# First sweep: two sums and two turns head a batch's mixing step, first-layer units from slot 5 on

## The chip, the cores and the metric

One Trainium2 chip, one core. The metric is the device time of one execution in microseconds (us). The kernel before takes 1207.25 us (median of three runs, 1206.75 to 1207.27). A measurement of this kernel tells apart about 0.2%.

## What is computed

Causal attention with a decay (8 batches, 8 heads, 576 positions, head width 64), then a mixer over its output: a sum along the sequence through `U` and `V` (rank 32), and a two-layer perceptron 512 to 2048 to 512 with a residual. Everything is float32.

```python
scores = scale * q @ k.T + (cum[:, None] - cum[None, :])   # causal mask
x  = softmax(scores) @ v                                   # heads side by side: (8, 576, 512)
u  = x + (x.T @ U @ V).T
out = u + relu(u @ w_ch1) @ w_ch2
```

## The kernel before, in words

**Two sweeps.** The first sweep (lines 778 to 946) does all of attention, pair of heads by pair of heads, and mixes in the first 6 of the 16 blocks of hidden channels of the perceptron (`NA = 6`). The second sweep, from line 950, does the other ten blocks from `ud`, a copy of `u` in DRAM. float32 operands of the large products are split in a high part (a cast, on ACT) and a low part (a subtraction, on DVE), and each product is three matmuls.

**Steps and slots.** The first sweep is a list of steps `t` (0 to 33), one for each of the 32 pairs of heads and two to run out; pair `p` is scored in step `p`. `step(t)` (L822) writes 10 slots `s`. Slots 0 to 3 and 6 to 9 hold a score tile each (`S14_02` is pair 14, head 0, row block 2), slots 4 and 5 the tail scores `St`; beside them stand the transposes of the exponentials of the pair before (`T`, slots 0 to 2 and 5 to 8), the product with the values (`V`, slots 0 and 7), and small ones (`Tx` slot 3, `Ty` slot 4, `Tt` slot 8). The order on PE and SP is as written; DVE, ACT and POOL are ordered by the scheduler when the program is built.

**Units.** A batch `b` has its last attention output at the end of step 4b+5. Step 4b+6 is its *mixing step* (`MIX`, L820): each slot pops one unit of `mix_units(b)` (L650), five sums `H` (`x + TS VV`, a 512-column matmul, added to `x` by DVE, L664), then four turns `Tu` and `Tv` (transposes of `u`; ACT copies the high half `uh`, L667, DVE subtracts for the low half `ul`, L668). The perceptron's units (`ffn_units`, L705) are the *filler*: first layer `A` (12 matmuls, L723; relu on ACT to `hh`, L732, low half `hl` on DVE, L728) and second layer `B` (6 matmuls, L742; three units to a sum, then added to `x` by DVE, L757). There are 24 units for an even batch and 27 for an odd one, in two groups of columns. The first group needs only the turns `Tu` 0 and 1. Six units are left over (`held`, L775) and run in slots 0 to 4 of the next mixing step; the others run in slots 1 to 6, 8 and 9 (`ROOM`, L936) of the three steps behind a mixing step, dealt out evenly by `credit` (L914 to L920).

**Banks.** `H`, `Tu`, `Tv`, `A` and `B` share the two banks of the pool `psF` (L107); a unit that opens a bank waits until the tile that held it was read for the last time: `H` by DVE (L664), `Tu` by ACT and then DVE (L668), `A` by ACT and then DVE (L728), `B` by DVE (L757). A `B` tile keeps its bank over three units, so that the units beside it have the other bank alone. The score tiles share the two banks of `psS` in turn: `S14_02` waits until ACT has read `S14_00` (the exponential `P14_00`, L394).

**When the evacuations are written.** `defer(phase, fn, slots)` (L266) puts them in the list of a later slot, by phase within it; ACT and DVE then get them in the scheduler's order.

Of the kernel before, what the change touches and what calls it, by code (L numbers as in the profile page):

```python
# [8 lines left out]
F32 = mybir.dt.float32  # L9
# [4 lines left out]
ALU = mybir.AluOpType  # L14
# [3 lines left out]
B, H, S, D = 8, 8, 576, 64  # L18
# [22 lines left out]
def tile_decay_attention_moe(ctx, tc, qk, v, f, U, V, w1, w2, out):  # L41
    nc = tc.nc
# [218 lines left out]
    filler = []  # L261
# [3 lines left out]

    def defer(phase, fn, slots=1):  # L266
        later.setdefault(now[0] + slots, []).append((phase, fn))

    def run_later():
        now[0] += 1  # L270
        for _, fn in sorted(later.pop(now[0], []), key=lambda x: x[0]):
            fn()

    def run_filler():
        w, fn = filler.pop(0)
        fn()
        return w
# [366 lines left out]
    fine = [0]  # L644
    share = [0.0]

    def charge(us):
        share[0] -= us

    def mix_units(b):  # L650
        X = xn[b % NX]
        units = []

        def bank(name):

            if b == B - 1:
                return psS.tile([P, 512], F32, tag="S", name=name)
            return psF.tile([P, 512], F32, tag="F", name=name)

        def hmix(i):  # L660
            kk = P if i < NM else TAIL
            ps = bank(f"H{b}_{i}")
            nc.tensor.matmul(ps[0:kk], VV[:, P * i : P * i + kk], TSb[b], start=True, stop=True)
            defer(4, lambda: (charge(0.6), nc.vector.tensor_tensor(X[0:kk, i], ps[0:kk], X[0:kk, i], op=ALU.add)))  # L664

        def evac_u(dh, dl, src):
            defer(3, lambda: nc.scalar.copy(dh, src))  # L667
            defer(1, lambda: (charge(0.6), nc.vector.tensor_tensor(dl, src, dh.bitcast(F32), op=ALU.subtract)), 2)  # L668

        def tu(i):  # L670
            if i == 0 and b % 2 == 0:
                cur[0] = sf.tile([P, NDC, 640], F32R, tag="uh", name=f"uh{b}")
                cur[1] = sf.tile([P, NDC, 640], F32R, tag="ul", name=f"ul{b}")
            uh, ul = cur
            tp = bank(f"Tu{b}_{i}")
            for c in range(NDC):
                nc.tensor.transpose(tp[:, P * c : P * c + P], X[:, i, P * c : P * c + P], ident)
            sl = slice(P * i, P * i + P)
            evac_u(uh[:, :, sl], ul[:, :, sl], tp.rearrange("p (c t) -> p c t", c=NDC))

        def tv():
            uh, ul = cur
            to = MAIN if b % 2 else MAIN + TAIL
            tp = bank(f"Tv{b}")
            for c in range(NDC):
                nc.tensor.transpose(tp[:, 64 * c : 64 * c + 64], X[0:64, NM, P * c : P * c + P], ident[0:64, 0:64])
            tv_ = tp[:, 0:256].rearrange("p (c t) -> p c t", c=NDC)

            evac_u(uh[:, :, to : to + TAIL], ul[:, :, to : to + TAIL], tv_)

            def use():
                for x, t in enumerate((uh, ul)):
                    if b < B - 1:
                        nc.sync.dma_start(ud[b, :, x], t.bitcast(F32)[:, :, 0:MAIN])
                    if b % 2:
                        jt = b // 2
                        nc.sync.dma_start(ud[B, :, x, :, P * jt : P * jt + P], t.bitcast(F32)[:, :, MAIN : MAIN + P])

            defer(4, use, 2)

        h = [(0.43, lambda i=i: hmix(i)) for i in range(NM + 1)]
        t = [(0.43, lambda i=i: tu(i)) for i in range(NM)] + [(0.25, tv)]
        return h + t

    def ffn_units(b):  # L705
# [3 lines left out]
        for t0, nt in groups:  # L709
            g = {}  # L710

            def l1(fc, t0=t0, nt=nt, g=g):
                uh, ul = cur
                if fc == 0:
                    g["hh"] = sf.tile([P, NA, 384], F32R, tag="hh", name=f"hh{b}_{t0}")
                    g["hl"] = sf.tile([P, NA, 384], F32R, tag="hl", name=f"hl{b}_{t0}")
                hh, hl = g["hh"], g["hl"]
                sl = slice(t0, t0 + nt)
                ps = psF.tile([P, 512], F32, tag="F", name=f"A{b}_{t0}_{fc}")
                m = 0  # L720
                for c in range(NDC):
                    for wt, ut in ((w1h, uh), (w1l, uh), (w1h, ul)):
                        nc.tensor.matmul(ps[:, :nt], wt[:, fc, c], ut[:, c, sl], start=m == 0, stop=m == 3 * NDC - 1)  # L723
                        m += 1

                def low():
                    charge(nt / 768)
                    nc.vector.scalar_tensor_tensor(  # L728
                        hl[:, fc, :nt], ps[:, :nt], 0.0, hh.bitcast(F32)[:, fc, :nt], op0=ALU.max, op1=ALU.subtract
                    )  # L730

                defer(3, lambda: nc.scalar.activation(hh[:, fc, :nt], ps[:, :nt], AF.Relu), 1 + fine[0])  # L732
                defer(1, low, 2 + fine[0])

            def l2(x, part, t0=t0, g=g):
                hh, hl = g["hh"], g["hl"]
# [38 lines left out]
    def held(t):  # L775
        return 4 if t > MIX[-2] else 6
# [36 lines left out]
    mixing = []  # L813
# [5 lines left out]
    LAST = len(SEQ) - 1  # L819
    MIX = [SEQ.index(NHP * b + NHP - 1) + 3 for b in range(B)]  # L820

    def step(t):  # L822
# [11 lines left out]
        for s in range(6 + 2 if last else SLOTS):  # L834
# [26 lines left out]
            if (t, s) in DECODES:  # L861
                u = DECODES.index((t, s))
# [42 lines left out]
            if px and s == (6 if last else 8):  # L905
                ranks(c)

            if mixing:
                for _ in range(2 if t == MIX[0] and s < 3 else 1):
                    mixing.pop(0)[1]()  # L910
                for _ in range(1 if ending else (1, 1, 2, 1, 1)[s] if s < 5 else 0):
                    if filler:
                        run_filler()
            elif len(filler) > held(t) and s in ROOM:  # L914

                ahead = sum(x >= s for x in ROOM) + len(ROOM) * (min(m for m in MIX if m > t) - 1 - t)
                credit[0] += (len(filler) - held(t)) / max(ahead, 1)
                if credit[0] > 0.999 or t > LAST - 3:
                    credit[0] = max(credit[0] - 1, 0)
                    run_filler()  # L920
            if ps_ and s == 6:
                score(p, 1, 0)
# [2 lines left out]
            if px and s == (6 + 1 if last else 9) and st[c]["hp"] == NHP - 1:  # L925
                b = st[c]["b"]
                assert len(filler) <= held(t) and not mixing
                mixing.extend(mix_units(b))
                nxt = ffn_units(b)
                pending.append(nxt)  # L930
            if not mixing and pending:
                assert not filler
                filler.extend(pending.pop())

    pending = []
    ROOM = (1, 2, 3, 4, 5, 6, 8, 9)  # L936
    credit = [0.0]
# [79 lines left out]
    for k, (_, _, _, joined, power, rest, whole, high, _) in enumerate(stages):  # L1017
        ahead = stages[k + 1][0:3] if k + 1 < len(wb) else ()
# [19 lines left out]
    with tc.manual_schedule(engines={ET.PE, ET.DVE, ET.Activation, ET.SP}):  # L1038
# [12 lines left out]
        h, t = ([fn for _, fn in x] for x in (mixing[0 : NM + 1], mixing[NM + 1 :]))  # L1051
        mixing = []
# [105 lines left out]
    ends = sf.tile([P, 2 * HT], F32, tag="TS", name="sum2")  # L1158
# [200 lines left out]
    held = {}  # L1359
# [289 lines left out]
```

## Time and profile before

| what | value |
|---|---|
| runs, device time | 1206.75, 1207.25, 1207.27 us |
| profiled execution, first to last instruction (span) | 1205.1 us; its device time isn't given, the median run is 2.15 us above the span |
| PE (matmul) busy | 1183.8 us, 98% of the span |
| DVE, ACT, POOL busy | 931.2 us (77%), 767.3 us (64%), 514.8 us (43%) |
| granted clock of TensorE | 1.00 in every slice |
| chain that ended last, by engine | PE 83%, DVE 8%, ACT 6% |

How to read it: a matmul's end is modelled, so a row's duration on PE overlaps the next one's; the time that PE spends on something is read from start to start. A gap that the view shows as idle is shorter than the time lost, by what the modelled end hides.

### The profile page before, as it was taken

The page shows a single profiled execution, that of the slowest core. Times are in us where ns is not written, and L with a number is a line of the kernel's source. Part 1 is how long each engine was busy: PE and PEld are TensorE (multiplying, and loading weights), DVE is VectorE, ACT ScalarE, POOL GpSimd, SP SyncE. Part 2 cuts the span into 40 slices and gives each one's busy share as a digit, 9 for nine tenths or more (in the row PEclk, how much of TensorE's full clock was granted, in tenths as well). Part 3 has the DMA queues.
Part 4 walks back from the last instruction along what each step waited for, and adds up shares of the span by engine and source line. Part 5 has one row for each costly group of instructions (what it writes and reads, how often), then busy time and mean ns, then how long its engine had stood idle before and what let it go on. Part 6 is the DMA issues. An engine that isn't in the chain of part 4 may idle for free.

```text
span 1205.1 us, 23859 instructions
## 1 busy us (share of the span) xinstructions
PE 1183.8 (98%) x8460; PEld 1084.9 (90%) x8460; DVE 931.2 (77%) x2233; ACT 767.3 (64%) x2076; POOL 514.8 (43%) x506
## 2 busy tenths in 40 slices
PE   8999999999999999999999999999999999999998
PEld 5888898998998988989989997788999999999998
DVE  8987878778778678877686699976777867778675
ACT  8877786776868758767766577434454544545543
POOL 2215463553635435544442000024575555555553
PEclk9999999999999999999999999999999999999999
DMA  5754244335335325425322244533424344243420
GB/s 161 192 139 146 81 104 155 103 82 160 84 89 169 102 69 152 121 69 172 90 79 90 97 144 160 159 105 94 134 86 110 101 133 134 96 115 99 132 52 36
DMA packets 81159, 138.47 MB, mean 115 GB/s; under 512 B 8752, under 2 KB 45616, under 8 KB 78992
## 3 DMA queue, kind: packets, MB, share of 16 engines
q1 hardware_dynamic: 79824, 128.56, 35.4%
q0 software_dynamic: 1152, 8.39, 3.8%
q8 instruction: 67, 1.10, 0.4%
q14 instruction: 52, 0.43, 0.1%
q10 hardware_dynamic: 64, 0.00, 0.0%
HBM read 101.08 MB, written 35.78 MB: 114 GB/s over the span
## 4 chain that ended last, share of the span: by engine, by line
PE 83%; DVE 8%; ACT 6%; issue 1%; POOL 0%; ACTq 0%; DVEq 0%; POOLq 0%
PE N L1283 12%; PE A L723 12%; PE B L742 11%; PE A L1263 9%; PE B L1263 7%; PE V L564 5%; PE T L461 4%; PE S L365 3%; PE V L536 3%; PE S L366 2%; PE B L1283 2%; PE Tt L630 2%; PE S L362 2%; PE O L1348 1%; ACT G L328 1%
## 5 line engine op out<-in xcount | busy, mean ns | idle before, releaser
L394 ACT ACTIVATE P<-S,nm 128x128 f32<-128x128 f32 (+3 forms) x256 | 139.0, 545 | 54.5 <-DVE nm L386 48.8
L197 POOL TENSOR_TENSOR hb<-xn,hb 128x256 fp32r<-128x256 f32 x136 | 113.6, 856 | 125.5 <-ACT hb L194 108.0
L386 DVE CUSTOM_DVE_ANT_0 S<-S,mask 128x128 f32<-128x128 f32 (+3 forms) x256 | 125.8, 496 | 52.3 <-PE S L366 46.3
L328 POOL CAST G<-qk 64x576 fp32r<-64x576 f32 x52 | 35.4, 680 | 206.9 <-PE St L366 150.4
L723 PE MATMUL A<-uh,w1h 128*128 128x256 f32 (+1 forms) x384 | 119.7, 312 | 0.0
L723 PE MATMUL A<-ul,w1h 128*128 128x256 f32 (+1 forms) x384 | 113.6, 296 | 0.0
L723 PE MATMUL A<-uh,w1l 128*128 128x256 f32 (+1 forms) x384 | 113.5, 296 | 0.0
L194 ACT CAST hb<-xn 128x256 fp32r<-128x256 f32 x136 | 51.8, 404 | 77.3 <-DVE xn L1269 42.8
L443 DVE TENSOR_TENSOR PTl<-T,PTh 128x512 fp32r<-128x512 f32 (+1 forms) x156 | 79.0, 527 | 12.1 <-ACT PTh L440 11.1
L742 PE MATMUL B<-w2h,hh 128*128 128x512 f32 x216 | 88.2, 408 | 0.0
L461 PE MATMUL T<-ident,P 128*128 128x128 f32 x544 | 85.5, 273 | 0.0
L344 POOL TENSOR_TENSOR G<-qk,G 64x576 fp32r<-64x576 f32 x52 | 74.6, 1434 | 24.6 <-ACT G L328 24.3
L742 PE MATMUL B<-w2l,hh 128*128 128x512 f32 x216 | 85.0, 394 | 0.0
L742 PE MATMUL B<-w2h,hl 128*128 128x512 f32 x216 | 84.6, 392 | 0.0
L1283 PE MATMUL N<-sw,hb 128*128 128x256 f32 x546 | 80.4, 283 | 0.0
L1283 PE MATMUL N<-b2h,hb 128*128 128x256 f32 x420 | 79.9, 282 | 0.0
L343 POOL TENSOR_TENSOR G<-qk,G 64x576 fp32r<-64x576 f32 x52 | 75.0, 1442 | 10.9 <-issue 4.2
L365 PE MATMUL S<-G 128*128 128x128 f32 x208 | 70.8, 345 | 7.0 <-ACT P L394 5.8
L723 PEld LDWEIGHTS A<-uh,w1h 128*128 128x128 f32 x384 | 72.9, 190 | 0.9 <-DVE hl L728 0.2
L723 PEld LDWEIGHTS A<-uh,w1l 128*128 128x128 f32 x384 | 73.1, 190 | 0.5
L723 PEld LDWEIGHTS A<-ul,w1h 128*128 128x128 f32 x384 | 72.8, 190 | 0.0
L1283 PEld LDWEIGHTS N<-sw,hb 128*128 128x128 f32 x546 | 71.7, 190 | 0.4 <-POOL hb L197 0.2
(328 smaller groups left out, 4006.3 us busy)
## 6 DMA issues: line engine op xcount, KB each, us to landing
qk<-in_qk_dram SPq DMA_DIRECT2D x104, 288.0 KB
direct<-ud SPq DMA_DIRECT2D x48, 256.0 KB
sr<-in_w_dram SPq DMA_DIRECT2D x20, 512.0 KB
vr<-in_v_dram SPq DMA_DIRECT2D x32, 256.0 KB
accd<-ost SPq DMA_DIRECT2D x32, 256.0 KB
xn<-accd SPq DMA_DIRECT2D x8, 1024.0 KB
out_dram<-xn SPq DMA_DIRECT2D x32, 256.0 KB
ud<-uh SPq DMA_DIRECT2D x7, 1024.0 KB
```

The lines of the kernel that those rows point to most:

```text
L197: leng.tensor_tensor(dl, src, dh.bitcast(F32), op=ALU.subtract)
L343: pin(el.tensor_tensor(g[oth, 2, cols], k[oth], gf[oth, 2, cols], op=ALU.subtract))
L344: pin(em.tensor_tensor(g[own, 1, cols], q[own], gf[own, 0, cols], op=ALU.subtract))
L365: nc.tensor.matmul(ps, G[j][:, 0, c0 : c0 + P], G[j][:, 2, cols], start=first, stop=False)
L386: newest["top"] = nc.vector.tensor_tensor_reduce(ps[:, :w], ps[:, :w], mask[:, 512 - w : 512], scale=-SCALE, scalar=3.0e38, op0=ALU.add, o ...
L394: nc.scalar.activation(pt, ps[:, :w], AF.Exp, bias=z["nm"][:, col : col + 1], scale=-1.0, accum_out=z["sm"][:, col : col + 1])
L443: defer(2, lambda: nc.vector.tensor_tensor(dstl, src, dsth.bitcast(F32), op=ALU.subtract))
L461: nc.tensor.transpose(tp[:, P * x : P * x + P], z["P"][j][i][:, P * c : P * c + P], ident)
L723: nc.tensor.matmul(ps[:, :nt], wt[:, fc, c], ut[:, c, sl], start=m == 0, stop=m == 3 * NDC - 1)
L742: nc.tensor.matmul(ps, ht[:, fc, P * x : P * x + P], wt[:, fc], start=fc == 0 and m == 0, stop=fc == NA - 1 and m == 2,)
L1263: nc.tensor.matmul(ps, a[x][:, c], b[y][:, c], start=start and m == 0, stop=m == 5, skip_group_check=not start)
L1283: nc.tensor.matmul(ps[:, y], a[p_][:, P * y : P * y + P], w[q_], start=start and y == 0 and m == 0, stop=stop and y == 1 and m == 2,)
```

## The change

The first 1008 matmuls of PE's order and all from number 4437 (of 8236) on stand as before; between them the same instructions stand in another order. `mix_units` orders the units of batches 1 to 6 as `H` 0, 1, `Tu` 0, 1, `H` 2, 3, 4, `Tu` 2, 3, `Tv`. The batch's perceptron units come into the filler behind slot 4 of its mixing step, and the slots 5, 6, 8, 9 of that step may take one each (`packed`). In those slots the low halves (`evac_u`, `l1`) are deferred a slot less, in phase 3. `credit` deals the units over the room of the mixing step's second half and the three steps behind it.

```diff
+    packed = [False]
+
+    def soon(slots, fn):
+        defer(*(3, fn, slots - 1) if packed[0] else (1, fn, slots))
+
...
         def evac_u(dh, dl, src):
             defer(3, lambda: nc.scalar.copy(dh, src))
-            defer(1, lambda: (charge(0.6), nc.vector.tensor_tensor(dl, src, dh.bitcast(F32), op=ALU.subtract)), 2)
+            soon(2, lambda: (charge(0.6), nc.vector.tensor_tensor(dl, src, dh.bitcast(F32), op=ALU.subtract)))
...
         t = [(0.43, lambda i=i: tu(i)) for i in range(NM)] + [(0.25, tv)]
+        if 0 < b < B - 1:
+            return h[0:2] + t[0:2] + h[2:] + t[2:]
         return h + t
...
-                defer(1, low, 2 + fine[0])
+                soon(2 + fine[0], low)
...
+            packed[0] = t in MIX[1:] and s > 4
             if mixing:
...
-            elif len(filler) > held(t) and s in ROOM:
-
-                ahead = sum(x >= s for x in ROOM) + len(ROOM) * (min(m for m in MIX if m > t) - 1 - t)
-                credit[0] += (len(filler) - held(t)) / max(ahead, 1)
-                if credit[0] > 0.999 or t > LAST - 3:
-                    credit[0] = max(credit[0] - 1, 0)
+            if (packed[0] or not mixing) and len(filler) > held(t) and s in ROOM:
+
+                ends = [6 if u == LAST else 9 for u in range(t, min(m for m in MIX if m > t))]
+                ahead = sum(x <= end and (n > 0 or x >= s) for n, end in enumerate(ends) for x in ROOM)
+                credit[0] += (len(filler) - held(t)) / ahead
+                if credit[0] > 0.999:
+                    credit[0] -= 1
                     run_filler()
...
-            if not mixing and pending:
+            if pending and (not mixing or (t, s) in [(m, 4) for m in MIX[1:]]):
                 assert not filler
                 filler.extend(pending.pop())
```

Units by slot, before and after, for batches 2 and 3 (an even and an odd one; `A`, `B` with a group's letter a or b, then the block or the row tile; `-` is a slot without a unit). Batches 4 and 6 go as 2 in the mixing step, 5 as 3; batch 1 as 3, but with its third `A` behind `Tv` in slot 9.

```text
step 14 before  H0+Bb0 | H1+Bb0 | H2+Bb0+Bb1  | H3+Bb1  | H4+Bb1 | Tu0   | Tu1   | Tu2 | Tu3    | Tv
step 14 after   H0+Bb0 | H1+Bb0 | Tu0+Bb0+Bb1 | Tu1+Bb1 | H2+Bb1 | H3+A0 | H4    | Tu2 | Tu3+A1 | Tv+A2
step 15 before  - | A0 | A1 | A2 | - | A3 | A4 | - | A5 | -
step 15 after   - | -  | A3 | -  | A4 | A5 | - | - | Ba0 | Ba0
step 16 before  - | Ba0 | Ba0 | Ba0 | - | Ba1 | Ba1 | - | - | Ba1
step 16 after   - | -   | Ba0 | Ba1 | - | Ba1 | Ba1 | - | - | Ab0
step 17 before  - | Ab0 | Ab1 | -   | Ab2 | Ab3 | Ab4 | - | - | Ab5
step 17 after   - | -   | Ab1 | Ab2 | -   | Ab3 | Ab4 | - | - | Ab5
step 18 after   H0+Bb0 | H1+Bb0 | Tu0+Bb0+Bb1 | Tu1+Bb1 | H2+Bb1 | H3+A0 | H4+A1 | Tu2 | Tu3+A2 | Tv
step 19 after   - | A3 | A4 | A5 | - | Ba0 | Ba0 | - | - | Ba0
```

Slot 1 of steps 15, 16, 17, 23, 24 and 25 held a unit and holds none; slot 1 of step 8, in front of the place from which the order differs, holds none in either.

**ACT, slots 2 to 4 of mixing step 14** (`P` exponentials, `PTh` high halves of turned exponentials, `uh` high half of a turn). Before:

```order
L440 CAST PTh13_3553<-T13_v_3606 128x128
L394 ACTIVATE P14_02_3631,sm14_3524<-S14_02_3603,nm14_3523 128x384
L394 ACTIVATE P14_03_3656,sm14_3524<-S14_03_3639,nm14_3523 128x512
L500 CAST PT413_3555<-Ty13_12_3669 64x128
L614 CAST xh12_3688<-xn0_104 128x640
```

After:

```order
L445 CAST PTh13_3553<-T13_v_3606 128x128
L399 ACTIVATE P14_02_3636,sm14_3524<-S14_02_3603,nm14_3523 128x384
L672 CAST uh2_3610<-Tu2_0_3612 128x4x128
L399 ACTIVATE P14_03_3665,sm14_3524<-S14_03_3644,nm14_3523 128x512
L672 CAST uh2_3610<-Tu2_1_3652 128x4x128
L505 CAST PT413_3555<-Ty13_12_3678 64x128
```

The high half of each of the first two turns now stands behind an exponential. `B1_256_1`, whose first unit ends slot 2, takes the bank that `Tu2_0` leaves; `H2_2` in slot 4 the one that `Tu2_1` leaves.

**DVE, slots 8 and 9 of mixing step 14** (`ISA ... nm14` the row minima of a score tile, `xT` the sum of the two halves of `V`, `ul` and `hl` low halves). Before:

```order
L386 ISA S14_12_3782,nm14_3523<-S14_12_3782,mask_93 128x384
L386 ISA nm14_3523 128x1
L584 TENSOR_TENSOR xT13_3755<-V13_0_3754,cr13_0_3756 64x576
L668 TENSOR_TENSOR ul2_3703<-Tu2_2_3768,uh2_3702 128x4x128
L443 TENSOR_TENSOR PTl13_3554<-T13_12_3785,PTh13_3553 128x256
L443 TENSOR_TENSOR PTl13_3554<-T13_12_3785,PTh13_3553 128x128
L386 ISA S14_13_3822,nm14_3523<-S14_13_3822,mask_93 128x512
```

After, from the same place:

```order
L391 ISA S14_12_3800,nm14_3523<-S14_12_3800,mask_93 128x384
L391 ISA nm14_3523 128x1
L589 TENSOR_TENSOR xT13_3773<-V13_0_3772,cr13_0_3774 64x576
L673 TENSOR_TENSOR ul2_3611<-Tu2_2_3786,uh2_3610 128x4x128
L448 TENSOR_TENSOR PTl13_3554<-T13_12_3803,PTh13_3553 128x256
L448 TENSOR_TENSOR PTl13_3554<-T13_12_3803,PTh13_3553 128x128
L642 TENSOR_TENSOR TS3_3807<-Tt12_3808,TS3_3807 32x128
L673 TENSOR_TENSOR ul2_3611<-Tu2_3_3818,uh2_3610 128x4x128
L391 ISA S14_13_3855,nm14_3523<-S14_13_3855,mask_93 128x512
L391 ISA nm14_3523 128x1
L735 SCALAR_TENSOR_TENSOR hl2_0_3715<-A2_0_1_3823,hh2_0_3714 128x256
L673 TENSOR_TENSOR ul2_3611<-Tv2_3858,uh2_3610 128x4x64
```

`A1` (`A2_0_1`) in slot 8 takes the bank of `Tu2_2`, and `A2` in slot 9 that of `A1`, whose low half stands behind the row minima of `S14_13`. In the odd batches `A1` follows `H4` in slot 6 and takes `H4`'s bank.

**PE, slots 1 and 2 of step 16.** Before:

```order
L461 MATMUL T15_01_4184<-ident_99,P15_03_3963 128x128
L742 MATMUL B2_0_0_4188<-w2h_109,hh2_0_3887 128x512
L742 MATMUL B2_0_0_4188<-w2h_109,hl2_0_3888 128x512
L742 MATMUL B2_0_0_4188<-w2l_110,hh2_0_3887 128x512
L742 MATMUL B2_0_0_4188<-w2h_109,hh2_0_3887 128x512
L742 MATMUL B2_0_0_4188<-w2h_109,hl2_0_3888 128x512
L742 MATMUL B2_0_0_4188<-w2l_110,hh2_0_3887 128x512
L365 MATMUL S16_02_4200<-G0_91 128x384
```

After:

```order
L371 MATMUL S16_01_4194<-G0_91 128x256
L466 MATMUL T15_01_4197<-ident_99,P15_01_3936 128x128
L466 MATMUL T15_01_4197<-ident_99,P15_02_3962 128x128
L466 MATMUL T15_01_4197<-ident_99,P15_03_3980 128x128
L370 MATMUL S16_02_4206<-G0_91 128x384
```

The unit between the transposes and `S16_02` is gone; it has moved to the end of step 15.

## Rows read from the trace of the kernel before

**Rows 1.** The page's first part: busy time and share of the span, TensorE.
```profile
PE 1183.8 (98%) x8460; PEld 1084.9 (90%) x8460; DVE 931.2 (77%) x2233; ACT 767.3 (64%) x2076; POOL 514.8 (43%) x506
```

**Rows 2.** Waits of PE, whole span: who waited for whom, us, times, longest.
```profile
PE S L365 <- ACT P L394: 5.8, 14, 0.9
PE Tv L686 <- DVE ul L668: 1.9, 6, 0.3
```

**Rows 3.** Busy time by engine, slot 6 of step 14 to slot 1 of 15.
```profile
281.10:293.20 12.10, 11.00 (x85) 9.34 (x84) 9.91 (x30) 11.79 (x33) 7.90 (x8) 1.00 0.44 115
```

**Rows 4.** Timeline of that stretch: start, duration, engine, instruction, [idle before <-releaser].
```profile
282.97 0.33 PE L365 MATMUL S<-G 128*128 128x128 f32 x1
...
283.46 0.39 PE L365 MATMUL S<-G 128*128 128x256 f32 x1
...
285.59 0.60 PE L677 MATMUL Tu<-ident,xn 128*128 128x128 f32 x4
...
286.41 0.44 PE L365 MATMUL S<-G 128*128 128x384 f32 x1 [0.21 <-ACT P L394]
...
286.87 0.49 PE L461 MATMUL T<-ident,P 128*128 128x128 f32 x3
...
287.38 0.28 PE L630 MATMUL Tt<-xh,Us 128*64 128x128 f32 x1
...
288.66 0.40 PE L366 MATMUL S<-G 128*128 128x512 f32 x1
...
289.38 0.43 PE L686 MATMUL Tv<-ident,xn 64*128 64x64 f32 x4 [0.32 <-DVE ul L668]
...
291.54 0.60 PE L461 MATMUL T<-ident,P 128*128 128x128 f32 x4
...
292.64 0.39 PE L365 MATMUL S<-G 128*128 128x256 f32 x1 [0.50 <-ACT P L394]
```

**Rows 5.** Timeline, PE, first half of step 14: like pairs that wait for nothing.
```profile
266.15 0.22 PE L365 MATMUL S<-G 128*128 128x128 f32 x1
...
266.32 0.68 PE L564 MATMUL V<-PTh,VS 128*128 128x448 f32 x3
...
272.43 0.49 PE L461 MATMUL T_v<-ident,P 128*128 128x128 f32 x3
...
272.67 0.48 PE L663 MATMUL H<-TS,VV 128*128 128x512 f32 x1
...
275.95 0.39 PE L366 MATMUL S<-G 128*128 128x512 f32 x1
...
276.19 0.60 PE L595 MATMUL Tx<-ident,xT 128*128 128x128 f32 x4
...
276.54 0.47 PE L663 MATMUL H<-TS,VV 128*128 128x512 f32 x1
```

**Rows 6.** Timeline, step 14: an exponential, a unit, row minima, a turn's high half.
```profile
273.38 0.60 ACT L394 ACTIVATE P<-S,nm 128x384 f32<-128x384 f32 x1
...
274.36 0.39 PE L742 MATMUL B<-w2h,hh 128*128 128x512 f32 x1
...
276.38 0.70 DVE L386 CUSTOM_DVE_ANT_0 S<-S,mask 128x512 f32<-128x512 f32 x1 [1.14 <-PE S L366]
...
283.28 0.60 ACT L667 CAST uh<-Tu 128x512 fp32r<-128x512 f32 x1
```

**Rows 7.** Groups by line, 200 to 860 us: xcount | busy us, mean ns | idle before.
```profile
L728 DVE SCALAR_TENSOR_TENSOR hl<-A,hh 128x256 fp32r<-128x256 f32 (+1 forms) x84 | 38.4, 457 | 11.5 <-ACT hh L732 11.3
...
L664 DVE TENSOR_TENSOR xn<-H,xn 128x512 f32<-128x512 f32 (+1 forms) x30 | 20.5, 685 | 1.5 <-PE H L663 1.4
...
L668 DVE TENSOR_TENSOR ul<-Tu,uh 128x512 fp32r<-128x512 f32 x25 | 17.0, 682 | 0.2 <-ACT uh L667 0.2
```

**Rows 8.** Timeline, PE, slots 1 and 2 of step 8.
```profile
141.05 0.49 PE L461 MATMUL T<-ident,P 128*128 128x128 f32 x3
...
142.43 0.44 PE L365 MATMUL S<-G 128*128 128x384 f32 x1 [0.89 <-ACT P L394]
```

## The prediction

> **What bounds the kernel now.** I read the page first: TensorE is busy 98% of the span [rows 1], so the first question is what of its order is lost time. The waits of PE come next: the score matmuls wait 14 times for ACT's exponentials, and `Tv` waits six times for a low half [rows 2]. Six is the number of mixing steps of batches 1 to 6, and the timeline puts these waits in the second half of those steps. From slot 6 of step 14 to slot 1 of step 15 ACT is busy 11.79 of 12.10 us, more than PE with 11.00, at a granted clock of 1.00 [rows 3]: here, and nearly only here, ACT and DVE are what PE waits for. In the first half of the step `B` units, which need no ACT, fill PE, and ACT has room.
>
> The loss is read from start to start, against like pairs in the first half, which wait for nothing. `S` of 128 columns to the next matmul: 0.49 us against 0.17; `Tu` to `S`: 0.82 against 0.35 for four transposes; three transposes to `Tt`: 0.51 against 0.24; `S` of 512 columns to `Tv`: 0.72 against 0.24; four transposes to `S15_01`: 1.10 against 0.35 [rows 4, 5]. Together 0.32 + 0.47 + 0.27 + 0.48 + 0.75 = 2.29 us in each mixing step, 13.7 us in six. That is all that filling these slots can give back; no instruction is added or removed, and the second sweep stands as it was.
>
> **The change, part by part.**
>
> *Given back.* Two turns leave the crowded half, which takes two `uh` copies off ACT there, and three `A` units of some 1.5 us each (12 matmuls) come in, each with one relu on ACT. PE is then the longer engine in that half, and the five waits close: 13.7 us. The most it can be is this; the least, if the first three stay, is (0.48 + 0.75) x 6 = 7.4.
>
> *New wait 1: `B1` in slot 2.* `B1` opens a bank, and the other bank is held by `B0`, so it takes the one that `Tu0` leaves, where before it took `H2`'s. The way to it is now: the exponential of `S14_02` starts at 273.38 and takes 0.60, ACT's copy `uh` behind it 0.60 [rows 6], DVE's `ul` 0.68 [rows 7], so 275.26, and about 0.1 for the handovers. PE was at this unit at 274.36 [rows 6] and comes some 0.1 later with a turn in place of a sum. PE waits 0.9. For the sum `H2` DVE alone was needed, and it ran beside `B0`. Six times 0.9 is 5.4 us (bounds: 0.6 to 1.2 each).
>
> *New wait 2: `H2` in slot 4* takes `Tu1`'s bank by the same way: the row minima of `S14_03` start 0.43 after its second matmul (275.95 to 276.38) and take 0.70 [rows 5, 6], the exponential some 0.7, `uh` 0.6, `ul` 0.68, with handovers 3.2 to 3.4 us. PE has some 3.0 us to spend: 0.24 and 0.35 [rows 5], 0.4 for `Tu1`, 1.4 for a unit of `B1` (272.67 to 274.36 less the sum's 0.3 [rows 5, 6]), the rest for the tail scores. I take 0.3, six times 1.8 (bounds 0 to 0.5 each).
>
> *New wait 3: `A1`.* In an odd batch it stands right behind `H4` and takes its bank: `H4` runs 0.47, DVE's addition 0.685 [rows 5, 7], and PE has only the rest of `H4` to do, 0.3; with a handover 0.9 us. In an even batch it takes `Tu2`'s bank in slot 8. No row shows this wait; the nearest is `Tv`'s for the same kind of low half, 0.48 [rows 4], which is the low end. Here the high half stands behind the copy of `V` on ACT, and `ul` behind the row minima of `S14_12` and `xT` on DVE, so I take 0.9, as in the odd batches. Six times 0.9 is 5.4 us (bounds 0.5 to 1.2).
>
> *New wait 4: `A2`.* In an even batch it takes `A1`'s bank, and DVE stands before the row minima of `S14_13`, which PE does behind `A1`: 0.43 + 0.70 + 0.46 for `hl` = 1.6 us after the second matmul of `S14_13` [rows 5, 6, 7], and PE has 0.24 and `Tv` to do, some 0.5. That is 1.1 us, though the low half was put a slot sooner in the list: DVE's order is the scheduler's. In batches 3 and 5 it waits for `ul` of `Tu2`, as `A1` did in the even ones, 0.8. In batch 1 it stands behind `Tv` and waits for `ul` of `Tu3`, which stands behind the minima of the 512-column tile, so the 1.6 and another turn's two halves less what PE does, an estimate of 2.2. Sum 3.3 + 1.6 + 2.2 = 7.1 us (bounds 4 to 9).
>
> *New wait 5: the empty slot 1.* `credit` now starts in the mixing step, and six steps (15, 16, 17, 23, 24, 25) lose the unit in slot 1. Step 8 shows what that costs: from the three transposes to `S8_02` 1.38 us against 0.24 [rows 5, 8], 1.1 us lost, because `S8_02` needs the bank of `S8_00`, whose exponential stands on ACT behind the copy of `V` and the split of the values. It is the longest wait of PE in [rows 2]. The same three instructions stand in that order in all six steps. 6 x 1.1 = 6.8 us (bounds 0.9 to 1.4 each).
>
> *Costed at nothing.* `A` and `B` units elsewhere only change slots: 18 or 21 a batch as before, with ACT and DVE less busy than PE around them. POOL's and SP's work of a slot is the same, and PE comes to it later rather than sooner. If a `B` unit loses the cover of an empty slot behind it, some 0.3 us.
>
> *The sum.* New waits 5.4 + 1.8 + 5.4 + 7.1 + 6.8 = 26.5 us, given back 13.7: +12.8 us on a span of 1205.1. The median run lies 2.15 above the span, so 1205.1 + 12.8 + 2.15 = 1220.1 us, **1220 us**. With every bound at its low end it is 3.6 + 0 + 3 + 4 + 5.4 = 16.0 less 13.7, +2.3 (1209.6); with every one at its high end 7.2 + 3 + 7.2 + 9 + 8.4 = 34.8 less 7.4, +27.4 (1234.7).
>
> Two rules stand on either side of this. The row says that in this half the engine with the most to do is ACT, 11.79 of 12.10 us [rows 3], and PE in the other. The Trainium skill's Perfetto Trace Analysis (Identifying Performance Opportunities, Optimization Strategy) says that where the most contended engine changes over time, interleaving the regimes may help. By it the 13.7 us come back and the bank waits are not there; that is the first rival. The row of `Tv` says that a unit which opens a bank waits for a low half, 0.32 us of listed idle time and 0.48 from start to start [rows 4]. The same page (Optimizing Tensor Performance, Matmuls) asks that independent groups rotate through PSUM banks, so that one's evacuation overlaps the next one's matmuls. The change does the contrary with two banks: it puts tiles with a two-engine evacuation beside a bank that is held. By this rule the waits 1 to 4 are there.
>
> **The rivals.** *Faster.* ACT and DVE serve the turns and `A` units in time, waits 1 to 4 stay under 0.2 us, and only the empty slots cost: 6.8 less 13.7, so 1200.3 us. For it speaks that ACT is idle between exponentials in slots 2 to 4; against it that each wait is a chain in order on two engines, where idle time helps nothing. It decides at wait 1: if `ul` of `Tu0` ends 0.9 us sooner than I have it, by standing before the exponential on ACT, there is no wait; the order written down has it behind.
>
> *Slower by half.* The chains are as I have them, but a wait early in the step gives ACT and DVE time to catch up, so that waits 3 and 4 shrink to half: 5.4 + 1.8 + 6.3 + 6.8 less 13.7, +6.6 and 1213.9 us. For it speaks that I added walks of one step, each from the state before; against it that `H4`'s and `A1`'s waits start from a matmul that PE itself has just done, which no delay before it shortens.
>
> *No change.* The waits add up to what is given back, so 1207; this needs all low ends and a little more.
>
> *A lower clock.* More pauses on PE could cost more than themselves if the granted clock fell to 1.2 GHz in the six half steps of 12.1 us [rows 3] and stayed there: their matmuls would take twice as long, at most 6 x 12.1 = 73 us on top of the waits, 1293 us. Step 8's pause of 0.89 us [rows 8] leaves the clock at 1.00 on the page, as all others do. The Trainium skill's TensorE: Matmul & The Clock Gate (A second HAM failure mode: psum-queue depth-cycling) tells of a kernel whose short pauses between groups on changing banks made the clock go back and forth; no row here shows a fall.
>
> **How the numbers follow.** The forecast (all waits, 1220) 0.62; slower by half 0.2; faster 0.1; no change 0.05; a lower clock 0.03. Of the first, most lies within 5 us. The range 1209 to 1229 leaves out the faster rival, the lower clock and no change, and the forecast's upper end. A measurement of this kernel tells 0.2%, 2.4 us, from no change; faster by more: 0.10, within: 0.05, slower by more: 0.85.
>
> **What would show it.** In the changed profile PE's waits should list `B L749 <- DVE ul` six times at up to 0.7 us, `A L730 <- DVE` at least six times (`xn`, `ul` or `hl`), and `S <- ACT P` still some ten times, now in steps 15 to 17 and 23 to 25, with `Tv <- ul` nearly gone. Step 14 should be longer by its three `A` units and by 1 to 2 us more. I am wrong if `B1` starts in slot 2 without a gap, if slot 1's wait is not in steps 16 and 17, or if DVE takes `hl` before the row minima of `S14_13`.

## The result and the profile after

The changed kernel takes 1220.3 us (median of four runs, 1219.44 to 1221.32) against 1207.0 us before (1206.69 to 1207.27): a ratio of 1.0111, with a 95% interval of 1.0096 to 1.0125. It is slower. The span of the profiled execution is 1217.7 us, 12.6 more than before; the prediction had 12.8. The median lies between two runs at a mean granted clock of 1.000 (spans 1217.7 and 1217.9 us) and two at 0.997 (1219.1 and 1219.5), so a gain against this kernel is given below by the spans of the profiled runs (all at 0.999 or 1.000) as well.

The page's first part, after:

```profile
PE 1183.2 (97%) x8460; PEld 1084.0 (89%) x8460; DVE 929.9 (76%) x2233; ACT 770.4 (63%) x2076; POOL 515.3 (42%) x506
```

The busy times are those of [rows 1] within half a per cent, so the 12.6 us are time in which PE waits. The waits of PE over the whole span (who waited for whom: us, times, longest) say for what:

```profile
PE S L370 <- ACT P L399: 6.9, 8, 0.9
PE A L730 <- DVE ul L673: 5.3, 6, 1.7
PE B L749 <- DVE ul L673: 4.3, 6, 0.9
PE A L730 <- DVE xn L669: 2.3, 3, 0.8
PE A L730 <- DVE hl L735: 2.2, 3, 0.7
```

The lines of the changed file lie a little further down: L365 of before is L370, L394 is L399, L663 to L668 are L668 to L673, L723 is L730, L728 is L735, L742 is L749. Against [rows 2], `Tv <- ul` is gone; of the 14 waits of `S` for `P` the twelve of the mixing steps (0.2 and 0.5 us each) are gone, two stay, and six of 0.89 us are new, one in each of the six empty slots 1; and three rows of `A` and one of `B` are new. `B` and the three `A` rows make 18 waits, three in each of the six mixing steps.

### The profile page after: what moved, and what is told of

It reads as the page before. It is cut to its first block, busy times and chain, and to the rows that moved or that the text cites. A ratio compares the mean times of both kernels' runs of the same rounds, so it can differ in the third digit from the quotient of the medians.

```text
span 1217.7 us, 23852 instructions
## 1 busy us (share of the span) xinstructions
PE 1183.2 (97%) x8460; PEld 1084.0 (89%) x8460; DVE 929.9 (76%) x2233; ACT 770.4 (63%) x2076; POOL 515.3 (42%) x506
## 4 chain that ended last, share of the span: by engine, by line
PE 82%; DVE 11%; ACT 4%; issue 2%; DMA 0%; POOL 0%; ACTq 0%; DVEq 0%; SPq 0%; POOLq 0%
PE N L1292 12%; PE A L730 12%; PE B L749 10%; PE A L1272 9%; PE B L1272 7%; PE V L569 6%; PE T L466 4%; PE S L370 3%; PE V L541 3%; PE S L371 2%; PE B L1292 2%; PE O L1357 2%; PE S L367 2%; DVE S L391 1%; PE Tt L635 1%
## 5 line engine op out<-in xcount | busy, mean ns | idle before, releaser
L399 ACT ACTIVATE P<-S,nm 128x128 f32<-128x128 f32 (+3 forms) x256 | 137.6, 540 | 63.0 <-DVE nm L391 56.7
L730 PE MATMUL A<-uh,w1h 128*128 128x256 f32 (+1 forms) x384 | 119.4, 311 | 9.9 <-DVE ul L673 5.3
L730 PE MATMUL A<-ul,w1h 128*128 128x256 f32 (+1 forms) x384 | 113.5, 296 | 0.0
L730 PE MATMUL A<-uh,w1l 128*128 128x256 f32 (+1 forms) x384 | 113.5, 296 | 0.0
L749 PE MATMUL B<-w2h,hh 128*128 128x512 f32 x216 | 89.9, 416 | 4.3 <-DVE ul L673 4.3
L749 PE MATMUL B<-w2l,hh 128*128 128x512 f32 x216 | 85.1, 394 | 0.0
L730 PEld LDWEIGHTS A<-uh,w1h 128*128 128x128 f32 x384 | 72.7, 189 | 13.5 <-PE Tu L682 4.6
L749 PE MATMUL B<-w2h,hl 128*128 128x512 f32 x216 | 84.7, 392 | 0.0
L370 PE MATMUL S<-G 128*128 128x128 f32 x208 | 69.8, 341 | 7.9 <-ACT P L399 6.9
L620 POOL TENSOR_TENSOR xh<-xn,xh 64x128 fp32r<-64x128 f32 x31 | 14.1, 456 | 149.0 <-ACT xh L619 140.0
L730 PEld LDWEIGHTS A<-uh,w1l 128*128 128x128 f32 x384 | 73.0, 190 | 0.7
L730 PEld LDWEIGHTS A<-ul,w1h 128*128 128x128 f32 x384 | 72.8, 190 | 0.0
```

The source lines that it names most:

```text
L370: nc.tensor.matmul(ps, G[j][:, 0, c0 : c0 + P], G[j][:, 2, cols], start=first, stop=False)
L399: nc.scalar.activation(pt, ps[:, :w], AF.Exp, bias=z["nm"][:, col : col + 1], scale=-1.0, accum_out=z["sm"][:, col : col + 1])
L749: nc.tensor.matmul(ps, ht[:, fc, P * x : P * x + P], wt[:, fc], start=fc == 0 and m == 0, stop=fc == NA - 1 and m == 2,)
```

## Each wait, read from its place

**`B1` in slot 2.** Timeline of step 14, changed kernel (start, duration, engine, instruction, idle before and releaser):

```profile
274.10 0.66 PE L682 MATMUL Tu<-ident,xn 128*128 128x128 f32 x4
...
275.08 0.58 ACT L399 ACTIVATE P<-S,nm 128x384 f32<-128x384 f32 x1 [0.28 <-DVE nm L391]
...
275.65 0.58 ACT L672 CAST uh<-Tu 128x512 fp32r<-128x512 f32 x1
275.75 0.40 PE L749 MATMUL B<-w2l,hh 128*128 128x512 f32 x1
276.26 0.69 DVE L673 TENSOR_TENSOR ul<-Tu,uh 128x512 fp32r<-128x512 f32 x1 [0.74 <-ACT uh L672]
...
277.00 0.50 PE L749 MATMUL B<-w2h,hh 128*128 128x512 f32 x1 [0.85 <-DVE ul L673]
```

These rows are the predicted chain: the exponential of `S14_02`, then `uh` behind it on ACT, then `ul` on DVE, then `B1`. The turn itself was there first: its row ends at 274.76, 0.3 us before that exponential begins, and ACT idles 0.28 us there; its copy stands behind in ACT's order. From start to start, the last matmul of `B0` to the first of `B1` is 1.25 us where 0.23 is usual: 1.02 us lost. In the odd batches it is 0.75, in six steps 5.3 us.

**`A1`, `A2` and slot 1.** Timeline of PE, changed kernel: steps 10 (batch 1), 14 (batch 2) and 15:

```profile
195.17 0.47 PE L668 MATMUL H<-TS,VV 128*64 128x512 f32 x1
196.42 0.38 PE L730 MATMUL A<-uh,w1h 128*128 128x256 f32 x1 [0.78 <-DVE xn L669]
...
203.10 0.43 PE L691 MATMUL Tv<-ident,xn 64*128 64x64 f32 x4
205.25 0.36 PE L730 MATMUL A<-uh,w1h 128*128 128x256 f32 x1 [1.72 <-DVE ul L673]
...
290.91 0.62 PE L682 MATMUL Tu<-ident,xn 128*128 128x128 f32 x4
292.32 0.36 PE L730 MATMUL A<-uh,w1h 128*128 128x256 f32 x1 [0.79 <-DVE ul L673]
...
294.05 0.40 PE L371 MATMUL S<-G 128*128 128x512 f32 x1
294.38 0.46 PE L691 MATMUL Tv<-ident,xn 64*128 64x64 f32 x4
295.58 0.39 PE L730 MATMUL A<-uh,w1h 128*128 128x256 f32 x1 [0.74 <-DVE hl L735]
...
298.80 0.60 PE L466 MATMUL T<-ident,P 128*128 128x128 f32 x4
299.15 0.36 PE L370 MATMUL S<-G 128*128 128x256 f32 x1
...
299.47 0.49 PE L466 MATMUL T<-ident,P 128*128 128x128 f32 x3
300.85 0.45 PE L370 MATMUL S<-G 128*128 128x384 f32 x1 [0.89 <-ACT P L399]
```

In step 10, `A1` stands right behind `H4`: 1.25 us from start to start against 0.31 when `H4` is followed by something that waits for nothing (so in the run with one unit in slot 5, below, 284.90 to 285.21), so 0.94. In step 14, `A1` stands behind `Tu3` and waits for `ul` of `Tu2`: 1.41 us for four transposes that otherwise take 0.35 to 0.4, so 1.03. `A2` follows `Tv` in both, 2.15 us behind its start in batch 1 and 1.20 in batch 2; before, what followed `Tv` came 0.36 us behind it, so 1.79 and 0.84 are lost. Two of the five places of [rows 4] stand here as well: the 512-column score tile to `Tv` takes 0.33 us (0.72 before), four transposes to `S15_01` 0.35 (1.10 before). The last pair is the empty slot 1: three transposes, and 1.38 us to `S15_02`, to the hundredth what step 8 showed before [rows 8]; the idle time listed is the same 0.89.

What DVE does ahead of the two waits of step 14 (timeline of DVE, same kernel; below it the relu of `A1`, timeline of ACT):

```profile
290.83 0.74 DVE L589 TENSOR_TENSOR xT<-V,cr 64x576 f32<-64x576 f32 x1
291.50 0.67 DVE L673 TENSOR_TENSOR ul<-Tu,uh 128x512 fp32r<-128x512 f32 x1
...
294.49 0.70 DVE L391 CUSTOM_DVE_ANT_0 S<-S,mask 128x512 f32<-128x512 f32 x1 [0.75 <-PE S L371]
...
295.10 0.42 DVE L735 SCALAR_TENSOR_TENSOR hl<-A,hh 128x256 fp32r<-128x256 f32 x1
```

```profile
294.02 0.39 ACT L739 ACTIVATE hh<-A 128x256 fp32r<-128x256 f32 x1 [1.14 <-PE A L730]
```

`ul` of `Tu2` stands behind `xT`, and `hl` of `A1` behind the row minima of `S14_13`, for which DVE itself waits 0.75 us. The relu that `hl` needs ends at 294.41, and DVE is idle until 294.49: there it is DVE's order, not its load, that holds the bank.

## The experiments

The theory was that the time is what PE loses, in its own order, to banks that two engines must empty one after the other, and to the empty slot 1; so each wait should go with its neighbours, and the gains should add. The main rival was that ACT and DVE are late as a whole, so that a wait taken away comes back elsewhere. All ratios are against the kernel before, with 95% intervals; "less" is against the changed kernel, by the medians and then by the spans.

**The order of sums and turns alone** (kernel before, one line more in `mix_units`):

```diff
+        if 0 < b < B - 1:
+            return h[0:2] + t[0:2] + h[2:] + t[2:]
         return h + t
```

> The kernel before with one part of the change alone: two sums and two turns head the mixing step; the first-layer units begin in slot 0 of the next step, as before, so slot 1 of the steps behind is filled, and no A unit stands among the sums and turns. Theory (PE waits for banks that two engines must empty): of the new waits only the one of B1 in slot 2 is there, 0.75 us in odd and 1.02 us in even batches as the changed kernel has it, 5.3 us in all; given back are surely the two waits that belong to the first turns of the crowded half, (0.32 + 0.47) x 6 = 4.7 us, and of the other three, 1.50 x 6 = 9.0 us, some part, since two copies of ACT have left. So 1207.0 + 5.3 - 4.7 less 0 to 9.0: 1199 to 1207.6, most likely 1203. Rival 1 (nothing hangs on B1's bank; the load of ACT and DVE is all that counts): no gap at B1 and all 13.7 us back, 1193. Rival 2 (the order of sums and turns is what costs, and the units moved into the step cost nothing): near the changed kernel, 1218 to 1220.

1211.74 us, ratio 1.0044 (1.0029 to 1.0059): outside the theory's 1199 to 1207.6, and neither rival's number. `B1`'s wait is there, six times, 0.75 us each. PE's waits (`B` is L744 in this file) in that run and, below them, the ends of one stretch in it (timeline of PE, step 14):

```profile
PE S L365 <- ACT P L394: 3.9, 8, 0.9
PE B L744 <- DVE ul L668: 3.5, 6, 0.6
PE S L365 <- ACT Ptl L422: 2.8, 7, 0.9
```

```profile
285.11 0.33 PE L365 MATMUL S<-G 128*128 128x128 f32 x1 [0.32 <-ACT Ptl L422]
...
294.07 0.39 PE L365 MATMUL S<-G 128*128 128x256 f32 x1 [0.39 <-ACT P L394]
```

From `S14_10` to `S15_01` PE does the same instructions here and before: 9.67 us before (282.97 to 292.64 [rows 4]), 8.96 here. So two turns fewer in that half give back 0.7 of the 2.29 us. `S15_01` still waits 0.39 us (0.50 before, [rows 4]), and `S14_10`, which didn't wait, now does, ahead of the stretch. From the step's first matmul to `S14_10` the step is 1.43 us longer: 0.75 at `B1`, 0.3 more than before at `S14_10` (it starts 0.80 us behind `H4`, where 0.31 is usual), the rest in pieces of about 0.1 at `H2` and where transposes and other matmuls take turns. So wait 1 stands, and what I had called sure of the gain, 4.7 us, was eaten by these.

**Slot 1 always filled** (changed kernel):

```diff
-                if credit[0] > 0.999:
-                    credit[0] -= 1
+                if credit[0] > 0.999 or (s == 1 and t > MIX[1]):
+                    credit[0] = max(credit[0] - 1, 0)
```

> The changed kernel, but slot 1 of every step behind the first mixing step of the sweep's batches always gets a unit, so that steps 15, 16, 17, 23, 24 and 25 have one there and an empty slot 2 instead of it in most. Theory (the exponential of S_00 stands on ACT behind the copy of V and the split of the values, so an empty slot 1 costs 1.13 us and another empty slot nothing much): six waits of 1.13 us gone, 1220.3 - 6.8 = 1213.5, and PE's waits for P fall from 8 to 2. Rival (an empty slot costs wherever it is, because ACT is late for the step as a whole): the waits move to slot 2 or 3 with some 0.7 to 1.1 us, 1218 to 1220.5.

1214.62 us, 1.0067 (1.0050 to 1.0083): 5.7 us less than the changed kernel, 4.6 by the spans. PE's waits of that run and, below them, slot 2 of step 15 and what follows (timeline of PE):

```profile
PE S L370 <- ACT P L399: 1.5, 2, 0.9
```

```profile
301.41 0.49 PE L466 MATMUL T_v<-ident,P 128*128 128x128 f32 x3
302.01 0.50 PE L370 MATMUL S<-G 128*128 128x512 f32 x1
```

Six of the eight waits are gone, as expected. Six empty slots 2 cost some 0.35 us each instead (three transposes to `S15_03` 0.60 us, where 0.25 is usual), 2.1 us: by the spans that is the missing part of the 6.8. So an empty slot costs in slot 2 as well, a third of what it does in slot 1.

**`B1` a slot later** (changed kernel):

```diff
-                for _ in range(1 if ending else (1, 1, 2, 1, 1)[s] if s < 5 else 0):
+                for _ in range(1 if ending else (1, 1, 1, 1, 2)[s] if s < 5 else 0):
```

> The changed kernel with its B units in the mixing step dealt 1, 1, 1, 1, 2 over slots 0 to 4 instead of 1, 1, 2, 1, 1, so that B1 opens its bank in slot 3, in B0's bank behind B0's evacuation, and Tu1 takes the bank that Tu0 leaves. Theory (a chain in order of exponential, uh and ul, whose length no idle time changes): Tu1 comes some 0.7 us later behind Tu0 than B1 did, by the rest of slot 2, so 0.2 us of the 0.9 is left, six times; H2 in slot 4 has the same cover as it had. 1220.3 - 4.1 = 1216. Rival (ACT and DVE have too much to do there, so the wait only moves): Tu1 or H2 waits 0.7 to 1 us instead, 1219 to 1221.

1214.84 us, 1.0066 (1.0051 to 1.0081), 5.5 us less, 5.4 by the spans: the theory's number and a little more. Timeline of PE, step 14, around `Tu1` and `B1` in slot 3:

```profile
275.41 0.60 PE L600 MATMUL Tx<-ident,xT 128*128 128x128 f32 x4
275.96 0.66 PE L682 MATMUL Tu<-ident,xn 128*128 128x128 f32 x4
276.55 0.50 PE L749 MATMUL B<-w2h,hh 128*128 128x512 f32 x1
```

`Tu1` comes 0.55 us after `Tx` where 0.35 to 0.43 is usual, and `B1` 0.2 late behind it: some 0.4 us of 1.02 are left, and the 0.10 that `H2` waited are gone. From step 13's `Tx` to step 15's, with the one mixing step between, PE takes 0.9 us less. PE has more to do while the chain runs.

**The `A` unit ahead of the sum or turn** in slots 5 to 9 (changed kernel; `deal` is the block that draws on `credit`):

```diff
+            if packed[0] and len(filler) > held(t) and s in ROOM:
+                deal()
             if mixing:
...
-            if (packed[0] or not mixing) and len(filler) > held(t) and s in ROOM:
+            if not packed[0] and not mixing and len(filler) > held(t) and s in ROOM:
+                deal()
```

> The changed kernel, but in slots 5 to 9 of a mixing step the A unit is issued ahead of the slot's sum or turn instead of behind it. Then A1 of an odd batch doesn't stand right behind H4, and in an even batch the turn of slot 8 has A1's 1.5 us ahead of it. Theory (waits 3 and 4 are made by what stands next to what): wait 3, 5.9 us, goes nearly all, of wait 4, 6.6 us, a part stays, since A2 of an even batch still needs the low half of A1; 1220.3 - 5.9 less 0 to 4: 1210.5 to 1214.5, most likely 1213. Rival (the half is bound by what ACT and DVE have to do, now that three relus and low halves are in it): the waits move to H4, Tu3 and Tv, which now take the banks of A units, and the time stays at 1218 to 1222.

1214.68 us, 1.0065 (1.0050 to 1.0080), 5.6 us less, 4.2 by the spans, just outside the theory's range. PE's waits, which held 18 of `A` and `B` before:

```profile
PE B L749 <- DVE ul L673: 4.3, 6, 0.9
...
PE A L730 <- DVE xn L669: 1.0, 3, 0.3
PE H L668 <- DVE xn L669: 1.0, 3, 0.3
```

The `A` rows shrink from 9.8 us in 12 waits to 1.0 in 3. What remains is new: `H4` or `A1` in slot 6 waits for the addition of `H3`, which stands just ahead, four transposes between (0.59 us lost each, 3.5 in all). Of the 11.9 us that waits 3 and 4 cost from start to start (table below) only 4.2 came back: besides those 3.5 us, some 4 stand in smaller pieces, in step 14 for instance 0.18 us at the transposes of slot 8 and 0.28 at `A2`, in batch 1 0.56 at `Tv`. Here the rival has a part: most of what was taken away at `A1` and `A2` came back beside them.

**Three waits taken away together**, with `A` ahead from slot 6 on only, and then slot 2 filled as well as slot 1 (these lines, with the other two edits; in the first of the two runs the condition is `s == 1`, and `t > NHP` fills step 8's slot 1 too):

```diff
-                if credit[0] > 0.999:
+                if credit[0] > 0.999 or s in (1, 2) and t > NHP:
...
+            first = packed[0] and s > 5
+            if first and len(filler) > held(t) and s in ROOM:
+                deal()
```

> The changed kernel with three of its four waits taken away together: slot 1 always gets a unit (from step 7 on, so in step 8 as well), the B units dealt 1, 1, 1, 1, 2, and from slot 6 on the A unit ahead of the slot's sum or turn (in slot 5 behind it, since H4 or A1 waited 0.59 us in slot 6 where it stood ahead in slot 5). Theory (the waits are separate, each made by its neighbours): the spans of the three single runs were 4.6, 5.4 and 4.2 us below the changed kernel's; with 1.1 for step 8 and 0.5 x 6 for slot 6 that is 18.3 us, so 1220.3 - 18.3 = 1202, 5 us under the kernel before. Rival (they share one cause, the load of ACT and DVE, and PE is late for the same work whichever wait is taken away): the gains don't add, 1208 to 1213.

> As the run with three waits taken away, but slot 2 always gets a unit as well as slot 1, so that empty slots fall on 3, 5, 7, 8 and 9. Theory: an empty slot 2 cost 0.35 us (0.5 + 0.5 of lost time in slots 2 and 3 against 0.3 + 0.35 with a unit), in some four steps, so 1 to 1.5 us less than that run, 1200.5. Rival (every empty slot costs about the same, except slot 1): no difference, 1202; or the empty slots 8 cost 0.4 and take it back.

1203.31 us, 0.9968 (0.9955 to 0.9981), and 1202.58 us, 0.9961 (0.9946 to 0.9976). The first has a span of 1201.6 us, 16.1 below the changed kernel's, of the 18.3 that the theory had: 14.2 that the three runs gave singly (4.6, 5.4 and 4.2) and 4.1 reckoned on top for step 8 and slot 6. The single gains are all there, so the three are separate from each other, and the rival that they share one cause falls (1208 to 1213). Filling slot 2 gives 0.7 us more, between the theory's 1 to 1.5 and the rival's nothing.

**One `A` unit, in slot 5** (changed kernel):

```diff
-            if (packed[0] or not mixing) and len(filler) > held(t) and s in ROOM:
+            if (s == 5 if packed[0] else not mixing) and len(filler) > held(t) and s in ROOM:
```

> The changed kernel, but of the mixing step's second half only slot 5 gets an A unit; the others begin in the step behind. Theory: waits 3 and 4 need A1 and A2 among the turns, so both go (5.9 + 6.6 = 12.5 us less); of what the A units gave back, the order alone kept 0.5 of 2.29 us a mixing step (the run with the order alone is 4.3 us of span longer than the kernel before at 0.75 us of B1's wait, six times), so three units gave back 1.8 and one of them may hold a third; 1.2 us, six times, comes back as waits, 7.2 us; empty slots 1 are now in steps 12, 16, 20, 24 and 28, five instead of six, 1.1 us less. 1220.3 - 12.5 + 7.2 - 1.1 = 1214. Rival 1 (what came back is due to the turns that left the half, not to the units put in): nothing of it is lost, 1207. Rival 2 (the units don't wait for each other, ACT and DVE are late as a whole): the waits move to H4 and the turns, 1219.

1209.56 us, 1.0018 (1.0009 to 1.0028): between the theory's 1214 and the 1207 of the first rival (the turns that left give it all back), and nearer to the rival's. The stretch from `S14_10` to `S15_01` says why (timeline of PE, step 14):

```profile
284.90 0.47 PE L668 MATMUL H<-TS,VV 128*64 128x512 f32 x1
285.21 0.22 PE L370 MATMUL S<-G 128*128 128x128 f32 x1
...
293.22 0.39 PE L370 MATMUL S<-G 128*128 128x256 f32 x1
```

8.01 us, against 8.96 with the order alone and 9.67 before. One unit gives back as much as 0.95 us; I had put a third of 1.8 on it. The last two runs below tell the unit's share from the turns'. The rows of `A` are gone from the waits, and `Tv` waits for `ul` six times again (2.0 us, as before); the seven waits for `P` that are left (6.0 us) hold the empty slots 1 of step 8 and of five others.

**The same with the other waits taken away**, once with `B1` in slot 3, once with three sums ahead of the first two turns and the unit in slot 6 ahead of `H4`; and the latter without its unit (of the edits, the line on the order):

```diff
-            return h[0:2] + t[0:2] + h[2:] + t[2:]
+            return h[0:3] + t[0:2] + h[3:] + t[2:]
```

> The run with an A unit in slot 5 alone, with two changes that took waits away on top: B units dealt 1, 1, 1, 1, 2 in the mixing step, and slots 1 and 2 always filled. Theory (one unit behind H3 gives back most of what three do and brings no wait, since no A unit then stands next to another tile that needs its bank): 1209.6 less 5.4 for B1's wait, less 6.0 for slots 1 (five steps and step 8), less 0.9 for slots 2: 1197.3. Rival (the second and third unit, once freed of their waits by being put first, are worth as much as the first): no better than the run with all three, 1201 to 1203.

> Wait 1 taken away in another way: three sums, two turns, two sums, two turns, the last turn, so that B1 opens in slot 2 in a sum's bank, as in the kernel before, and the first turns stand in slots 3 and 4; one A unit, in slot 6 ahead of H4, where the turns' halves are there; slots 1 and 2 always filled. Theory (it is the turn's bank, emptied by ACT and then DVE, that B1 waits for): no gap at B1; Tu1 in slot 4 takes Tu0's bank with a unit of B1, 1.4 us, and the tail scores between them, as H2 did in the changed kernel without a wait: some 5 us less than the run with one unit in slot 5 less its empty slots, 1196 to 1199. Rival (the turn's evacuation costs its 0.75 us wherever the turn stands): Tu1 or H3 waits as long as B1 did, 1201 to 1203.

> The run with three sums and two turns at the head, without its A unit in slot 6: the order of sums and turns and the filled slots 1 and 2 alone. Theory (one A unit gives PE something to do while ACT and DVE finish the exponentials, and that is where the gain comes from): of the 2.29 us that the second half of a mixing step loses in the kernel before, the run with the order alone kept 1.8, and the run with one unit here has about 0.9 us a mixing step less lost time in slots 6 to 0 than that: 5.4 us come back, 1197.9 + 5.4 = 1203. Rival (the gain is that of the order and of the filled slots, and the A unit's place is worth nothing): 1197.5 to 1199.

1198.20 us, 0.9932 (0.9917 to 0.9947); 1197.87 us, 0.9929 (0.9912 to 0.9945); and without the unit 1204.68 us, 0.9984 (0.9974 to 0.9993). The first two are as the theory has it; the third is 1.7 us above its 1203 and far from the rival's 1197.5 to 1199. Timeline of PE in the run of 1197.87 us, step 14, slots 2 to 4 and the ends of the stretch read above:

```profile
270.08 0.48 PE L668 MATMUL H<-TS,VV 128*128 128x512 f32 x1
...
271.54 0.39 PE L749 MATMUL B<-w2l,hh 128*128 128x512 f32 x1
271.77 0.39 PE L749 MATMUL B<-w2h,hh 128*128 128x512 f32 x1
...
274.03 0.60 PE L682 MATMUL Tu<-ident,xn 128*128 128x128 f32 x4
...
276.62 0.55 PE L682 MATMUL Tu<-ident,xn 128*128 128x128 f32 x3
...
281.79 0.22 PE L370 MATMUL S<-G 128*128 128x128 f32 x1
...
289.81 0.39 PE L370 MATMUL S<-G 128*128 128x256 f32 x1
```

`B1` follows `B0` after 0.23 us: it takes a sum's bank, which DVE alone empties. `Tu1` stands 2.6 us behind `Tu0` and doesn't wait for it. Without the unit in slot 6 the stretch takes 8.95 us instead of 8.02 (timeline of PE in that run):

```profile
282.43 0.33 PE L370 MATMUL S<-G 128*128 128x128 f32 x1 [0.32 <-ACT Ptl L427]
...
291.38 0.39 PE L370 MATMUL S<-G 128*128 128x256 f32 x1 [0.38 <-ACT P L399]
```

In all 6.8 us are lost, 1.1 a mixing step. So the order alone is worth little, and one unit is what gives the half its time back.

**The kernel before with slot 1 of step 8 filled:**

```diff
-                if credit[0] > 0.999 or t > LAST - 3:
+                if credit[0] > 0.999 or t > LAST - 3 or (t, s) == (8, 1):
```

> The kernel before with one unit more: slot 1 of step 8, its one empty slot 1 among steps with units, gets one, and the units behind move by up to a slot. Theory (wait 5's mechanism is there in the kernel before): 1.1 us less, 1205.7, too small for the time alone to tell, so the trace has to show that S8_02 no longer waits. Rival (the wait is step 8's own and goes to another slot): 1206.8 and a wait of P elsewhere in step 8.

1206.59 us, 0.9997 (0.9988 to 1.0007): the time can't tell. In the trace (timeline of PE, step 8) a `B` unit stands ahead of `S8_02`, which starts 0.23 us behind the unit's last matmul, so the wait is gone there too:

```profile
142.52 0.39 PE L742 MATMUL B<-w2l,hh 128*128 128x512 f32 x1
142.75 0.34 PE L365 MATMUL S<-G 128*128 128x384 f32 x1
```

Not run: the low halves at their old place. Undoing `soon` leaves the instructions of all five engines in the changed kernel's order, row for row, so this part of the change does nothing, as the prediction had for `A2`. Nor was the copy `uh` of the first turn put ahead of the exponential on ACT, which would show by itself what ACT's order costs at `B1`.

## Why the prediction was right

| term | predicted, us | measured, us | from |
|---|---|---|---|
| given back | -13.7 | -13.0 | four of the five places of [rows 4] at their usual times in all six steps; `Tv` 0.09 late in five, 0.30 in batch 1 |
| wait 1, `B1` | 5.4 | 5.3 | 1.02 in three steps, 0.75 in three |
| wait 2, `H2` | 1.8 | 0.6 | 0.10 in each of six |
| wait 3, `A1` | 5.4 | 5.9 | 0.94 and 1.03, three each |
| wait 4, `A2` | 7.1 | 6.0 | 0.84 x 3, 0.86 x 2, 1.79 in batch 1 |
| wait 5, slot 1 | 6.8 | 6.8 | 1.13 x 6 |
| sum | +12.8 | +11.6 | span: +12.6 |

1.0 us of the span's growth stand with no term: pieces of 0.2 to 0.35 us, in slot 8 of steps 15 and 23 and at the end of slot 2 of step 31 among them. (The expectations of two runs have wait 4 at 6.6 us; from start to start, with 0.36 for `Tv`, it is 6.0.)

- **The mechanism held.** Each bank wait is where it was put, with the engine and operation named ahead, and a change of what stands beside it took it away, at `A1` and `A2` wholly only where the second and third unit left the step. `hl` came behind the row minima of `S14_13`, as DVE's order had it.
- **Wait 2 was sized wrong.** The step "DVE and PE race to `Tu1`'s bank, 3.2 to 3.4 us against 3.0" gave 0.3; it is 0.1.
- **Wait 4** was put at 7.1 and is 6.0: 0.84 against 1.1 in the even batches, 1.79 against 2.2 in batch 1.
- **The sum is closer than its terms**, and that is luck: `H2` and `A2` were put 2.3 us too high; against that `A1` was 0.5 too low, 0.7 less was given back, and 1.0 stand with no term.
- **"Given back" had its reasons in the wrong proportion.** The prediction named two: turns that leave the half, and `A` units that come in. The runs show 0.7 us of a mixing step for the turns (0.4 when the new wait at `S14_10` is taken off) and 0.95 for the first unit.
- **The rivals.** "Faster" fell at `B1`, as it said it would: `ul` ended 0.97 us after PE was there. "Slower by half" fell: waits 3 and 4 kept 11.9 of the 12.5 us that they were put at. In the profiled run the granted clock stayed at 1.00 through a pause of 1.72 us.
- **The two rules.** Interleaving the regimes does give back what the crowded half lost; the trace agrees with the Trainium skill's Perfetto Trace Analysis (Identifying Performance Opportunities, Optimization Strategy), and the run of 1197.87 us earns it. The other rule, of the Trainium skill's Perfetto Trace Analysis (Optimizing Tensor Performance, Matmuls), is that independent groups rotate through PSUM banks so that one's evacuation overlaps the next one's matmuls. The trace agrees: where the next unit came to a bank of the two that was still being emptied, PE lost 17.8 us in waits 1 to 4, more than was given back.

## What to carry to other kernels

When work is moved to fill an engine that waits, look at what it will stand next to: with two banks, a tile needs the bank of a tile one or two places ahead of it, and the one to watch is a tile that two engines empty in turn, behind whatever stands ahead of it in their orders. One unit of filler at a place where its bank is long free gave back nearly 1 us a step; the second and third, put beside tiles that need the bank at once, cost 2 us. An empty slot isn't free either: find which of them cover an evacuation (here slot 1, 1.13 us, and slot 2, 0.35) and leave others empty.

## What the runs showed that was not expected

The waits hardly interact: taken away together they gave 16.1 us, and 14.2 singly, though ACT is busy 11.19 of 14.60 us in that half (windows view of the changed kernel, slot 6 of step 14 to slot 1 of step 15; columns as in [rows 3]; below it about the same stretch, without slot 1, in the run of 1197.87 us):

```profile
286.30:300.90 14.60, 12.18 (x100) 11.03 (x98) 10.18 (x31) 11.19 (x32) 6.99 (x7) 1.00 0.44 118
...
281.00:289.90 8.90, 8.57 (x72) 7.71 (x70) 7.73 (x24) 8.79 (x26) 5.15 (x6) 1.00 0.42 103
```

In the fastest run ACT is busy 8.79 of 8.90 us there, PE 8.57. That speaks for ACT's own work as the bound of the half by then; no run here takes work off ACT in it, so this isn't shown.
